# Rows of step 10 between step 11's scores, and expert 0's second half ahead of the fills of list and gates

## The chip, the cores and the metric

The kernel runs on one core of a Trainium2 chip. The metric is the device time of one execution in microseconds (us): the median of the runs of a kernel. Engines are named as in the profile: PE (TensorE, the matrix products), DVE (VectorE), ACT (ScalarE), POOL (GpSimd), SP (SyncE, which here only issues DMAs).

## What is computed

Three layers follow each other. A gated linear recurrence over 768 positions for 4 x 8 heads of 48 lanes; its rows, 3072 tokens of 384 values, go through a layer in which a score lets a token skip and an argmax sends every other token to one of eight experts; the result goes through a dense layer with SiLU.

```python
def _attn_ref(q, k, v, a_re, a_im):          # per batch and head, state S of 48 x 48
    ...
        S_re, S_im = (new_re + kv, new_im)   # decayed state plus outer product of k and v
        y[:, :, t] = np.einsum('bhd,bhde->bhe', q[:, :, t], S_re)

def _moe_ref(x, w_skip, w_gate, w1, w2):
    do_compute = x @ w_skip > 0
    xc = x[do_compute]
    logits = xc @ w_gate
    e_idx = np.argmax(logits, axis=1)
    ...                                      # gate_w: softmax of the chosen logit
    for e in range(E):
        mask = e_idx == e
        h = np.maximum(xc[mask] @ w1[e], 0.0)
        y[mask] = gate_w[mask, None] * (h @ w2[e])
    out[do_compute] = xc + y

def _moe2_ref(x, w_in, w_out):
    h = x @ w_in
    return ((h * (1.0 / (1.0 + np.exp(-h)))) @ w_out)
```

## The kernel before

The recurrence is worked in chunks of 128 positions. There are 12 steps: six chunks, each in two halves of two batches (b = 0 and 1). A step of attention ends with scores of keys and queries (`scores`, in four groups of four heads, `sc00`, `sc10` of batch 0, `sc01`, `sc11` of batch 1), a mask on DVE (`scores_out`), products with values and state (`value`), a copy `yT` on ACT (`value_out`), four transposes back to rows (`rows`, into the PSUM bank `px`), a copy `xr` (`rows_out`) and a DMA of these rows to the buffer xbuf in DRAM (`store`, on SP). After steps 1, 3, ... 11 the logits of the chunk are formed from `yT` (`logits`).

From the logits the router makes, on DVE and PE, a list: which token stands in which of 16 slots of 128 (two per expert). It does so in two parts, r0 for the first 16 groups of 128 tokens and r1 for the last 8. Per part: pick the expert (`e1`/`l1`), rank the token (a product), mark the slot, a one-hot matrix `hot` (`l4`), the fills of the list (`l6`, products slots<-r1bt,r1hot), the softmax weight (`y1` to `y6`) and the fills of the gates (`y7`, slots<-r1bg,r1hot). `slot_tokens` (`l7`) turns the list into `gidx`, by which POOL gathers the rows of each slot from xbuf.

Expert 0's first tile of 128 tokens comes from the list of r0 alone, and is worked inside the attention phase: `gather0`, `turn0`, up products of two halves in two pieces each (`up0`; `f4`, `p4` for the first half, `f5`, `p5` for the second), Relu on ACT (`relu0`; `f6`, `f8`), the low part on DVE (`relu0_lo`; `f7`, `f9`), products with the second weights (`down0`; `fa`, `pa`, each 12 products) and a copy `y0` (`fb`). The hidden values of the second half lie in the attention buffers cs and sn, those of the first in kn.

After it the expert phase begins (`dense`). Its first steps on PE: filler products on a matrix of ones (`idle`), the transposes of expert 0's second tile, again filler products, its up products (`up_one`) with the transposes of expert 1's two tiles between them, and its products `down_last`, which need Relu `hh` (ACT) and the low part `hl` (DVE). Weights of an expert come as four loads of 768 KB on SP (`load`), each cast on ACT (`whole`) and subtracted on DVE (`lower`). The two loads of expert 1's first weights go to a pool whose memory lies on the attention buffers; the second must wait until `down0` has read cs and sn.

What sets the order: within the attention phase each piece of work has a number in a table (PLACE, one for each of the 12 steps, and TAIL for the router and expert 0's first tile). All pieces are sorted by that number and written in that order, so every engine has its instructions in the order of the numbers. In the expert phase each piece has a due time worked out from a few constants, and the table SHIFT moves single ones. Each engine works strictly in its own order, and waits at an instruction until what it reads is there.

Of the kernel before, what the change touches and what calls it, by code (L numbers as in the profile page):

```python
# [105 lines left out]
    "flip": (0, 323, 0, 443, 0, 581, 0, 671, 0, 803, 0, 839),  # L106
    "lgb": (0, 344, 0, 462, 0, 632, 0, 677, 0, 805, 0, 841),
# [10 lines left out]
}  # L118
ENG = {
    "z": "VGVVVGGVGGVV", "qe": "VGGVGVVVGVVG", "ks": "GVVGVGGGVVVV", "kc": "GVVGGGVVVGVG", "qc":  # L120
# [18 lines left out]

SHIFT = {  # L140
# [4 lines left out]
}  # L145
# [1624 lines left out]
```

## Time and profile before

| | before |
|---|---|
| median of 3 runs | 775.18 us (774.18 to 775.31) |
| profiled execution | 778.0 us, span 776.2 us from first to last instruction |
| mean granted clock of PE | 0.988 of full |

The page gives for each engine its busy time. Below it the chain of work that ended last is followed back; most of it is PE. The rows shown further down are from views of the trace in order of time: start in us from the span's start, duration, engine, source line, operation, output and inputs with buffer numbers left out, count, and in brackets how long the engine sat idle before it and what ended that wait. A product of two float32 operands is recorded more than once, so counts of PE can be a multiple of those in the code.

### The profile page before, as it was taken

What the parts mean: (1) busy time and instruction counts of PE and PEld (TensorE: products, weight loads), DVE (VectorE), ACT (ScalarE), POOL (GpSimd) and SP (SyncE); (2) the same over time, 40 slices, a digit from 0 to 9 for tenths busy, and PEclk for the clock granted to TensorE, in tenths of its full rate; (3) what the DMA queues carried; (4) which work ended last, traced back from release to release, by engine and by line L of the source; (5) the groups of instructions that cost most, each with busy time, mean ns of one, the idle gap of its engine ahead of it and who ended that gap; (6) DMA issues with size and microseconds to landing.
All of it is one profiled execution on the core that took longest, in us unless ns stands there. A gap on an engine that the chain in (4) does not pass through costs nothing.

```text
span 776.2 us, 13953 instructions
## 1 busy us (share of the span) xinstructions
PE 741.5 (96%) x5499; PEld 683.1 (88%) x5499; DVE 536.1 (69%) x957; ACT 437.9 (56%) x718; POOL 211.0 (27%) x193
## 2 busy tenths in 40 slices
PE   3799999999999999999999999999999999999995
PEld 2699999998988999998999899988888888888885
DVE  7899889999754867579898243654565556556544
ACT  7899899955424654454676212344555455555443
POOL 4478567223523134224300037810000000000000
PEclk9799999999999999999999999999999999999998
DMA  8567787587837865657660011001000101101001
GB/s 345 166 199 234 243 267 235 158 230 224 277 108 274 293 238 211 225 202 229 213 215 34 1 41 41 1 31 44 9 30 12 42 1 41 41 1 42 1 1 45
DMA packets 31530, 101.87 MB, mean 131 GB/s; under 512 B 4960, under 2 KB 13536, under 8 KB 31456
## 3 DMA queue, kind: packets, MB, share of 16 engines
q1 hardware_dynamic: 26128, 88.05, 34.6%
q0 software_dynamic: 3072, 9.44, 3.3%
q10 hardware_dynamic: 2256, 3.41, 1.3%
q8 instruction: 45, 0.74, 0.4%
q14 instruction: 29, 0.24, 0.1%
HBM read 69.27 MB, written 12.58 MB: 105 GB/s over the span
## 4 chain that ended last, share of the span: by engine, by line
PE 78%; DMA 10%; DVE 3%; ACT 2%; issue 2%; SPq 2%; POOL 1%; DVEq 0%; POOLq 0%; ACTq 0%
PE ph L936 29%; PE py L936 25%; PE pd L936 6%; PE sc L483 4%; DMA xbuf<-xg,sidx 4%; DMA KQ<-o 3%; PE run L310 2%; PE pu L516 2%; PE py L501 2%; SPq L447 2%; PE py L505 2%; PE tp L473 1%; PE pt L1349 1%; PE px L533 1%; DMA raw<-in_w_dram 1%
## 5 line engine op out<-in xcount | busy, mean ns | idle before, releaser
L936 PE MATMUL ph<-cxh,wh 128*128 128x512 f32 x288 | 113.6, 395 | 0.0
L936 PE MATMUL ph<-cxl,wh 128*128 128x512 f32 x288 | 112.9, 392 | 0.0
L936 PE MATMUL ph<-cxh,wl 128*128 128x512 f32 x288 | 112.6, 391 | 0.0
L1214 DVE TENSOR_TENSOR gl<-g,gh 128x512 fp32r<-128x512 f32 x64 | 44.3, 692 | 89.1 <-ACT gh L1213 45.3
L1212 ACT ACTIVATE g<-ph 128x512 f32<-128x512 f32 x64 | 38.2, 597 | 49.4 <-PE ph L936 49.2
L936 PEld LDWEIGHTS ph<-cxl,wh 128*128 128x128 f32 x288 | 54.0, 188 | 11.6
L936 PEld LDWEIGHTS ph<-cxh,wl 128*128 128x128 f32 x288 | 54.1, 188 | 9.2
L936 PEld LDWEIGHTS ph<-cxh,wh 128*128 128x128 f32 x288 | 54.2, 188 | 9.0
L1234 ACT CAST tz<-twd 128x256 fp32r<-128x256 f32 x96 | 36.7, 407 | 42.2 <-DVE twd L1226 42.1
L1019 DVE TENSOR_TENSOR wl<-raw,wh 128x1536 fp32r<-128x1536 f32 x28 | 48.5, 1752 | 11.7 <-ACT wh L917 11.7
L483 PE MATMUL sc<-KQ 96*128 96x128 f32 x384 | 52.3, 285 | 0.0
L483 PEld LDWEIGHTS sc<-KQ 96*128 96x128 f32 x384 | 47.7, 198 | 1.6 <-issue 1.4
L917 ACT CAST wh<-raw 128x1536 fp32r<-128x1536 f32 x28 | 40.7, 1480 | 13.2 <-DMA raw<-in_w_dram 13.2
L936 PE MATMUL ph<-xh,wh 128*128 128x240 f32 x168 | 46.5, 277 | 0.0
L936 PE MATMUL ph<-xl,wh 128*128 128x240 f32 x168 | 46.1, 275 | 0.0
L936 PE MATMUL ph<-xh,wl 128*128 128x240 f32 x168 | 46.1, 275 | 0.0
L1051 POOL DMA_INDIRECT xbuf<-xg,sidx x16 | 21.7, 1356 | 84.5 <-DMA xbuf<-xg,sidx 41.4
L936 PE MATMUL py<-wh,gl 128*128 128x384 f32 x128 | 43.2, 338 | 0.0
L936 PE MATMUL py<-wh,gh 128*128 128x384 f32 x128 | 43.1, 337 | 0.0
L936 PE MATMUL py<-wl,gh 128*128 128x384 f32 x128 | 43.0, 336 | 0.0
L936 PE MATMUL py<-wh,hh 128*128 128x384 f32 (+1 forms) x120 | 41.7, 348 | 0.0
L936 PE MATMUL py<-wh,hl 128*128 128x384 f32 (+1 forms) x120 | 41.0, 342 | 0.4 <-DVE hl L1036 0.3
(374 smaller groups left out, 2117.4 us busy)
## 6 DMA issues: line engine op xcount, KB each, us to landing
raw<-in_w_dram SPq DMA_DIRECT2D x30, 768.0 KB, 5.9
KQ<-o SPq DMA_DIRECT2D x40, 290.2 KB, 3.8
kq<-in_kq_dram SPq DMA_DIRECT2D x12, 768.0 KB, 5.1
a<-in_a_dram SPq DMA_DIRECT2D x10, 768.0 KB, 6.5
raw<-in_w_in_dram SPq DMA_DIRECT2D x8, 768.0 KB, 4.9
raw<-in_w_out_dram SPq DMA_DIRECT2D x8, 768.0 KB, 4.3
v<-in_v_dram SPq DMA_DIRECT2D x12, 384.0 KB, 6.1
xbuf<-xr SPq DMA_DIRECT2D x24, 192.0 KB, 2.9
```

Source lines behind the costliest of these rows:

```text
L310: nc.tensor.matmul(p[:, i if bank is None else bank, g * CH:g * CH + CH], a[:, n * CH:n * CH + CH], tri, start=first and g == 0, stop=last ...
L447: nc.sync.dma_start(t.KQ[every(2 * d0 + half, n, 2), h0:h0 + ng, b], o[every(p0, n, step), g0:g0 + ng])
L483: nc.tensor.matmul(sc[:, j, :], key(4 * g + j), t.KQ[0:96, 4 * g + j, b, 1, 0:CH], start=True, stop=True)
L501: nc.tensor.matmul(py[64 * i:64 * i + 64, j, :], t.v[:, v0 + h * D:v0 + h * D + DP], u.P[:, h, :], start=True, stop=first)
L505: nc.tensor.matmul(py[64 * i:64 * i + 64, j, :], state[0:96, s0 + h * D:s0 + h * D + DP], t.KQ[0:96, h, b, 1, 0:CH], start=False, stop=True)
L917: nc.scalar.copy(hi, src)
L936: nc.tensor.matmul(out, a, x, start=first and n == 0, stop=last and n == len(pairs) - 1)
L1019: nc.vector.tensor_tensor(u.w[i][1], u.raw[i], u.w[i][0].bitcast(F32), ALU.subtract)
L1051: nc.gpsimd.indirect_dma_start(out=k.x, out_offset=bass.IndirectOffsetOnAxis(ap=k.sidx[:, c:c + 1], axis=0), in_=u.xg[i], in_offset=None)
L1212: nc.scalar.activation(a, u.ph[f], AF.Silu)
L1214: tt(u.gl[f], a, u.gh[f].bitcast(F32), ALU.subtract)
L1234: nc.scalar.copy(h, u.x[:, n])
```

## The change

Two groups of numbers are altered. Transposes, copy and store of step 10 (`row`, `xr`, `st`) get places among the scores of step 11, the deferred store of step 9 goes in front of them, and step 11's second rows and both its stores come a little earlier. In TAIL the second half of expert 0's first tile (`p5`, `f8`, `f9`, `pa`) gets places ahead of the fills of the list (`l6`, 868) and of the gates (`y7`, 878). In SHIFT the cast and the subtraction of expert 1's first load get 1.7 us more.

```diff
-    "row0": (211, 275, 327, 400, 502, 545, 610, 647, 721, 775, 862, 843),
-    "xr0": (233, 298, 329, 404, 520, 553, 616, 654, 727, 779, 864, 845),
-    "st0": (316, 469, 446, 432, 543, 668, 624, 748, 787, 865, 876, 863),
+    "row0": (211, 275, 327, 400, 502, 545, 610, 647, 721, 775, 817.5, 843),
+    "xr0": (233, 298, 329, 404, 520, 553, 616, 654, 727, 779, 817.7, 845),
+    "st0": (316, 469, 446, 432, 543, 668, 624, 748, 787, 830.1, 830.2, 852),
...
-    "row1": (204, 258, 373, 408, 522, 560, 704, 684, 742, 784, 846, 857),
-    "xr1": (210, 267, 390, 421, 539, 562, 709, 703, 753, 789, 851, 861),
-    "st1": (378, 407, 482, 505, 667, 577, 729, 736, 764, 802, 855, 881),
+    "row1": (204, 258, 373, 408, 522, 560, 704, 684, 742, 784, 822.5, 846),
+    "xr1": (210, 267, 390, 421, 539, 562, 709, 703, 753, 789, 822.7, 851),
+    "st1": (378, 407, 482, 505, 667, 577, 729, 736, 764, 802, 830.4, 855),
...
-    867, "l6": 868, "p5": 869, "f7": 870, "f8": 871, "l7": 872, "y6": 873, "yb": 874, "fa": 875, "f9": 877,
-    "y7": 878, "y8": 879, "pa": 880, "fb": 882,
+    867, "l6": 868, "p5": 862.5, "f7": 870, "f8": 863.5, "l7": 872, "y6": 873, "yb": 874, "fa": 875, "f9": 872.5,
+    "y7": 878, "y8": 879, "pa": 876.5, "fb": 882,
...
-    "E1 lower 3": 2, "E1 relu_lo 0": 1, "E1 whole 1": 0.2, "E2 lower 1": 4.65, "E2 turn 0": -0.4,
+    "E1 lower 0": 1.7, "E1 lower 3": 2, "E1 relu_lo 0": 1, "E1 whole 0": 1.7, "E1 whole 1": 0.2, "E2 lower 1": 4.65, "E2 turn 0": -0.4,
```

On PE, at the scores sc of step 11 (KQ_144 are its keys and queries, px the transposes to rows):

```order
 L505 MATMUL py<-KQ_143,state 64x128 x2
-L483 MATMUL sc<-KQ_144 128x128 x16
+L483 MATMUL sc<-KQ_144 128x128 x4
+L533 MATMUL px<-ident,yT 128x128 x4
+L483 MATMUL sc<-KQ_144 128x128 x8
+L533 MATMUL px<-ident,yT 128x128 x4
+L483 MATMUL sc<-KQ_144 128x128 x4
 L501 MATMUL py<-P_2581,v_139 64x128 x2
```

The two groups of transposes of step 10 now stand behind the first and the third group of scores.

On PE, where the list is filled (slots<-r1bt,r1hot; ph_2747 and ph_2760 are the second half up of expert 0's first tile, py its products, of which the first rows are shown):

```order
-L533 MATMUL px<-ident,yT 128x128 x4
-L926 MATMUL ph_2747<-KQ_143,raw 128x128 x6
-L533 MATMUL px<-ident,yT 128x128 x4
+L926 MATMUL ph_2760<-KQ_143,raw 128x128 x12
 L836 LDWEIGHTS r1hot
 L836 MATMUL slots<-r1bt,r1hot 128x32
...
-L926 MATMUL ph_2747<-KQ_143,raw 128x128 x6
-L936 MATMUL py_2802<-wh,kn_2745 128x384
...
+L936 MATMUL py_2806<-wh,kn_2758 128x384
```

Both pieces of the second half up stand in front of the fills of the list, and no transposes are left there. The 24 products py now follow the list's fills in one piece, and the fills of the gates, which stood between the first and the second 12, come behind them.

On ACT, from the last copies of rows to the Relu hh of expert 0's second tile (y is the copy of the first tile's result, xh the second tile's rows, wh the casts of expert 1's first two loads):

```order
-L248 COPY xr_2755<-px 128x384
-L248 COPY xr_2763<-px 128x384
-L658 ACTIVATE cs<-ph_2747 128x512
-L705 COPY y_68<-py_2802 128x384
-L917 CAST wh<-raw 128x1536
+L658 ACTIVATE cs<-ph_2760 128x512
+L705 COPY y_68<-py_2806 128x384
 L1061 COPY xh<-pt 128x3x128
-L917 CAST wh<-raw 128x1536
+L917 CAST wh<-raw 128x1536 x2
 L1071 ACTIVATE hh<-ph 128x512
```

The copy xh now stands ahead of both casts, and hh behind both, as before.

On DVE the low part sn of the second half moves from behind the chain of the gates to a place right behind gidx. On SP the five stores of rows keep their place between the loads of expert 0's and expert 1's weights; their order among themselves changes from step 10, 11, 9, 10, 11 to 9, 10, 10, 11, 11. POOL's order stays.

## Rows read from the trace of the kernel before

**Rows 1.** The page, part 1: busy time, share of the span, instructions

```profile
PE 741.5 (96%) x5499; PEld 683.1 (88%) x5499; DVE 536.1 (69%) x957; ACT 437.9 (56%) x718; POOL 211.0 (27%) x193
```

**Rows 2.** PE in order of time, 214 to 233 us: start, duration, work

```profile
214.25 0.55 PE L649 MATMUL tp<-ident,xg 128*128 128x128 f32 x3
...
223.60 0.66 PE L533 MATMUL px<-ident,yT 128*128 128x128 f32 x4 [0.41 <-ACT xr L248]
224.09 1.50 PE L926 MATMUL ph<-KQ,raw 128*128 128x128 f32 x12
225.43 0.60 PE L533 MATMUL px<-ident,yT 128*128 128x128 f32 x4
225.87 0.59 PE L836 MATMUL slots<-r1bt,r1hot 128*128 128x32 bf16 x8
...
227.64 0.42 PE L936 MATMUL py<-wh,kn 128*128 128x384 f32 x1
...
229.82 0.37 PE L836 MATMUL slots<-r1bg,r1hot 128*128 128x48 bf16 x8
230.03 0.42 PE L936 MATMUL py<-wh,cs 128*128 128x384 f32 x1
...
232.24 0.95 PE L983 MATMUL pt<-ones 128*128 128x128 bf16 x14
```

**Rows 3.** DVE in order of time, 224 to 230 us

```profile
224.85 1.29 DVE L827 TENSOR_TENSOR r1hot<-i,r1rest 128x512 bf16<-128x512 f32 x2
...
226.84 0.17 DVE L867 TENSOR_TENSOR gidx<-base,slots 128x16 uint32<-128x16 f32 x1
...
228.92 0.56 DVE L791 TENSOR_TENSOR r1bg<-r1oc,r1g 128x384 bf16<-128x384 f32 x1
```

**Rows 4.** SP's queue in order of time, 232 to 234 us

```profile
232.43 0.34 SPq L1013 DMA_DIRECT2D raw<-in_w_dram  x1
```

**Rows 5.** POOL in order of time, 207 to 233 us: gathers

```profile
207.31 1.18 POOL L642 DMA_INDIRECT xg<-xbuf,gidx  x1 [0.52 <-DVE gidx L861]
...
229.80 0.97 POOL L990 DMA_INDIRECT xg<-xbuf,gidx  x1 [14.43 <-DVE r1bg L791]
...
232.32 0.94 POOL L990 DMA_INDIRECT xg<-xbuf,gidx  x1 [0.30 <-issue]
```

**Rows 6.** DMA issues at 207.3, 227.4, 232.43, 232.3 us: size, us to landing

```profile
xg<-xbuf,gidx POOLq DMA_INDIRECT x1, 5.9
...
raw<-in_w_dram SPq DMA_DIRECT2D x1, 768.0 KB, 4.2
...
raw<-in_w_dram SPq DMA_DIRECT2D x1, 768.0 KB, 6.3
xg<-xbuf,gidx POOLq DMA_INDIRECT x1, 6.6
```

**Rows 7.** ACT and DVE in order of time, 238 to 243 us

```profile
238.78 1.47 ACT L917 CAST wh<-raw 128x1536 fp32r<-128x1536 f32 x1 [4.12 <-DMA raw<-in_w_dram]
...
242.02 0.68 DVE L931 SCALAR_TENSOR_TENSOR hl<-ph,hh 128x512 fp32r<-128x512 f32 x1
```

**Rows 8.** PE in order of time, 234 to 243 us: expert 0's second tile

```profile
234.72 2.94 PE L926 MATMUL ph<-xh,raw 128*128 128x128 f32 x24 [0.30 <-ACT xh L1061]
...
239.07 0.52 PE L1002 MATMUL pt<-ident,xg 128*128 128x128 f32 x3 [1.08 <-DMA xg<-xbuf,gidx]
...
242.03 0.42 PE L936 MATMUL py<-wh,hh 128*128 128x384 f32 x1
...
242.76 0.44 PE L936 MATMUL py<-wh,hl 128*128 128x384 f32 x1
```

**Rows 9.** PE in order of time, 360 to 361 us: group 0's transposes

```profile
360.70 1.39 PE L1349 MATMUL pt<-ident,xr 128*128 128x128 f32 x6 [1.41 <-DMA xr<-xbuf,order]
```

**Rows 10.** Two stretches: length, busy by engine, granted clock, DMA share, GB/s

```profile
236.00:244.00 8.00, 6.77 (x54) 6.25 (x54) 3.78 (x6) 3.32 (x5) 2.84 (x3) 1.00 0.76 244
360.00:366.00 6.00, 5.21 (x22) 5.02 (x23) 4.79 (x8) 3.06 (x5) 1.72 (x2) 0.72 0.42 165
```

## The prediction

> **What bounds the kernel now.** The page comes first: TensorE (PE) is busy for 741.5 us [rows 1] of a span of 776.2, so only work taken off PE, or a wait of PE, can move the end; DVE, ACT and POOL matter through the waits that they cause. The change takes no product away, so the question is which waits of PE it ends. Second view, PE in order of time in the stretch that the change edits, from the last scores of attention to expert 0's second tile. Three places are to be seen there. PE waits 0.41 us in front of the transposes at 223.60, for ACT to empty the bank px. The products py of expert 0's first tile begin at 227.64, are cut by the fills of the gates (229.82 to 230.03), and the next work begins at 232.24 [rows 2]. Behind that PE waits 0.30 us for ACT's xh, 1.08 us for a gather, and at the second tile's products it starts the first at 242.03 but the third only at 242.76 [rows 8].
>
> Third, what stands behind that last wait. SP issues the second load of expert 1's weights at 232.43 [rows 4], the moment at which the products py of the first tile end: the load's buffer lies on cs and sn, which these products read. It lands 6.3 us later [rows 6], ACT casts it at 238.78 with all later work of ACT behind it, and DVE's hl, which the third product needs, begins at 242.02 [rows 7]. So the chain is: end of py, load 6.3, then 238.75 to 242.76, 4.0 us of cast, subtraction and hl. PE has work in parallel, but less of it than this chain is long. The end of py decides.
>
> **The change, part by part.** The time that I work against is the profiled execution's, 776.2 us of span and 778.0 in all; the runs shown have a median of 775.18. The saving in us is put on that median.
>
> *Rows of step 10 between the scores.* Two groups of four transposes px move from behind (225.43 to 225.87 is 0.44 each [rows 2]) to between the four groups of scores. PE has no wait there, so everything behind them, up to the transposes of step 11, is 0.88 later. The logits are among it, and so the whole list chain on DVE: its last step, r1hot, ended at 224.85 + 1.29 = 226.14 [rows 3] and will end at 227.02.
>
> What it gives: the transposes of step 11 no longer share the bank px with step 10's in that stretch, so the wait of 0.41 goes. PE starts expert 0's second half up at 224.09 + 0.88 - 0.44 - 0.41 = 224.12, as before (224.09 is where the transposes of 223.60 ended). Now both pieces run in one, 2 x 1.34 (224.09 to 225.43 [rows 2]), to 226.80. The first four list fills take 0.2, and PE comes to the second four at 227.0, when r1hot is just there. The cover is used up exactly: any later r1hot is a wait of PE. The fills end at 227.3, products py start at 227.35 instead of 227.64: 0.29 earlier.
>
> *Relu and subtraction of the second half earlier, products in one piece.* Relu on ACT follows the up products at 226.8, sn on DVE follows gidx and ends near 228.5; PE needs it 2.2 us after 227.35, at 229.5. No wait. The chain of the gates on DVE is pushed back by the 0.88 and by sn (0.6 in line): r1bg ended at 229.48 [rows 3] and ends near 231.0. PE comes to these fills at 227.35 + 2 x 2.2 = 231.75, so again nothing, with 0.7 us to spare. As these fills (0.21, 229.82 to 230.03 [rows 2]) now stand behind the products and not in them, the products end 0.29 + 0.21 = 0.50 earlier: the second load leaves at 231.93 instead of 232.43.
>
> *Stores earlier.* SP's queue was held by the first of five stores until step 11's rows were copied; now three of them leave during step 11's scores, beside the gather of the first tile. That gather left at 207.31 [rows 5] and took 5.9 [rows 6], so it was there at 213.2, and PE wanted it at 214.25, now at 215.1 [rows 2]. Below: no loss. Above: the slowest gather among my rows took 6.6 [rows 6], which gives 213.9. No cost. The other gathers waited for the last of these stores to land. It now leaves near 224.4 (step 11's transposes end at 223.75, the copy takes 0.5) and has 3.5 us until the list is there, so they wait for the list alone: gidx ends at 227.01 + 0.88 = 227.9, the first gather leaves at 228.2 instead of 229.80, the third (expert 1's second tile) 2.5 later, 230.7 instead of 232.32 [rows 3, 5]. Even with its 6.6 us it is there at 237.3; PE would want it at 239.07 - 1.08 - 0.30 - 0.29 = 237.4. The wait of 1.08 ends.
>
> *Cast of expert 1's first half behind xh on ACT.* ACT took the cast (1.47 [rows 7]) first and xh behind it; with the order turned, xh is ready while PE still runs its filler products, and the 0.30 goes. The cast itself has no reader before the subtraction on DVE, 2 us before the next one needs DVE.
>
> *What is late next.* PE's own work from 232.24 to 242.03 is 9.79 less the waits 0.30 and 1.08, 8.41. From 231.95 it is at the second tile's products at 240.36, and without a wait the third would be at 240.8. But hl comes by the chain: 231.93 + 6.3 + 4.0 = 242.26. Of the 1.38 us saved on the way nothing reaches the end; PE waits them again, as one wait of some 1.5 us, and the third product is 0.50 earlier than before.
>
> The one price that the rows of before don't fix is the second load's landing. It took 6.3 with gathers leaving 0.1 before it and every 1.25 us behind it; the first load of the pair took 4.2 [rows 6]. After the change the gathers are 1.6 earlier and the load 0.5, so again one leaves at almost the same moment (231.95) and others follow at the same pace. The nearest row is thus the load itself, and I take 6.3; bounds are 4.2 and 7 (a little over the 6.6 of the gather beside it).
>
> The Trainium skill (DMA: Bandwidth & Descriptors, section on the anatomy of one DMA) gives a fixed 2.0 us plus bytes over 436 GB/s, by which I estimate 3.8 us for these 768 KB. The first load's 4.2 nearly agrees, the second's 6.3 does not, and by the page's figure alone hl would not be what PE waits for, as in the second case below.
>
> Sum: 0.50 us earlier at the third product. Behind it I see no wait of PE that is worth a term until the 1.41 at 360.70 [rows 9], and loads, casts and scatters there are started by work that moves along. 775.18 - 0.50 = 774.7; the profiled execution by the same sum has a span of 775.7.
>
> **The rivals.**
>
> *The load lands sooner.* If it is back in 4.2 us, it lands at 236.1 and hl is ready at 240.1, before PE comes. Then PE alone decides, and the third product is at 240.8, 1.96 earlier: 773.2. For it: fewer gathers are left to follow the load, since they began 1.6 earlier, and expert 2's load is held longer by the later subtraction. Against it: at 231.95 the fourth gather leaves just as the third did at 232.32.
>
> *The gain is taken back later.* At 360.70 PE has waited 1.41 us for the last gather of group 0's rows [rows 9], which ends POOL's long chain of scatters and gathers, each waiting for a landing. If that chain keeps its time while PE comes 0.5 earlier, PE waits 0.5 longer there, and the time is 775.2. The same comes out if r1hot or the load is half a us late. Against it: expert 1's scatters start that chain, and they follow PE.
>
> *A clock that falls.* Behind that wait of 1.41 the granted clock fell from 2.4 to 1.2 GHz for a while: the mean over 360 to 366 is 0.72, so 6 x 0.28 = 1.7 us of full clock were lost. From 236 to 244 it stayed at 1.00 [rows 10], with the 1.08 of rows 8 as the longest wait. The change joins the waits into one of 1.5, longer than the one that was followed by the fall. If the clock falls there too, the time is 774.7 + 1.7 = 776.4, slower than before; with a load of 7 us the wait grows to 2.2 and the time to 777.1. [...] Against it: around that one PE had another wait and only a few transposes, here products stand on both sides.
>
> That the change doesn't do what it says I give no weight of its own: if r1hot is so late that the products don't begin earlier, it is the second rival.
>
> **How the numbers follow.** Forecast 0.50, at 774.7 (774.2 to 775.2 for a landing of 5.8 to 6.8); sooner landing 0.23, at 773.2; taken back 0.14, at 775.2; clock 0.13, at 776.4. 0.2% is 1.55 us, about what a measurement of this kernel can tell from no change: faster means below 773.6, slower above 776.7. The sooner landing gives nearly all of faster, 0.22; of the clock's case about half, with a late load, goes over the upper bound, and some part of what I have not seen: 0.09; the rest, 0.69, is within. The range is 773.0 to 776.5: it takes in the full gain below and a fall of the clock above.
>
> **What would show it.** Right: the transposes of step 10 stand between scores; no wait for xr behind the rank; products py in one piece from about 227.3; the second load issued near 231.9; no wait for the gather; one wait of about 1.5 us inside the second tile's products, ended by hl; the third product near 242.3. Wrong: a landing of that load under 5.5 or over 7 us; a wait of more than 0.3 us for r1hot or r1bg; a granted clock below 1 between 236 and 250; a wait at group 0's transposes that differs by more than 0.5 us from before.

## The result and the profile after

| | before | after |
|---|---|---|
| median, 13 runs each | 775.18 us (773.73 to 777.03) | 780.14 us (775.74 to 783.39) |
| ratio, 95% interval | | 1.0058 (1.0043 to 1.0073) |
| profiled execution: span | 776.2 us | 777.9 us |

By the medians the change makes the kernel 5 us slower, where 0.5 us faster was forecast (774.7, range 773.0 to 776.5). In this set its runs also spread more than twice as far; in a later set the kernel before spread as far, from 771.7 to 780.7. A ratio is the measurement's own, over the runs that were not disturbed, and can differ a little from the quotient of two medians.

The page of after, part 1, answers [rows 1]: PE has the same work.

```profile
PE 742.3 (95%) x5499; PEld 684.3 (88%) x5499; DVE 538.1 (69%) x957; ACT 437.9 (56%) x718; POOL 208.8 (27%) x193
```

PE of after in order of time, from the scores of step 11 to the third product of expert 0's second tile; it answers [rows 2, 8].

```profile
209.79 0.60 PE L533 MATMUL px<-ident,yT 128*128 128x128 f32 x4
...
212.01 0.60 PE L533 MATMUL px<-ident,yT 128*128 128x128 f32 x4
...
223.52 0.60 PE L533 MATMUL px<-ident,yT 128*128 128x128 f32 x4
...
224.12 2.92 PE L926 MATMUL ph<-KQ,raw 128*128 128x128 f32 x24
226.88 0.67 PE L836 MATMUL slots<-r1bt,r1hot 128*128 128x32 bf16 x8
...
227.40 0.42 PE L936 MATMUL py<-wh,kn 128*128 128x384 f32 x1
...
231.81 0.37 PE L836 MATMUL slots<-r1bg,r1hot 128*128 128x48 bf16 x8
232.03 0.94 PE L983 MATMUL pt<-ones 128*128 128x128 bf16 x14
232.80 0.50 PE L1002 MATMUL pt<-ident,xg 128*128 128x128 f32 x3
233.14 0.94 PE L983 MATMUL ph<-ones 128*128 128x128 bf16 x14
239.64 5.22 PE L926 MATMUL ph<-xh,raw 128*128 128x128 f32 x24 [5.56 <-ACT xh L1061]
...
247.95 0.42 PE L936 MATMUL py<-wh,hh 128*128 128x384 f32 x1
...
248.38 0.35 PE L936 MATMUL py<-wh,hl 128*128 128x384 f32 x1
```

Down to 233.14 it goes as forecast. Then PE sits for 5.56 us in front of the second tile's up products, waiting for ACT's copy xh, where it waited 0.30 before. The products themselves take 5.22 us instead of 2.94. The third product comes at 248.38, 5.62 later than in before.

Who held xh up: ACT, DVE, SP and POOL of after in order of time.

```profile
232.01 0.48 ACT L705 COPY y<-py 128x384 f32<-128x384 f32 x1 [4.26 <-issue]
239.11 0.48 ACT L1061 COPY xh<-pt 128x384 f32<-128x384 f32 x1 [6.62 <-remote]
...
233.28 0.21 DVE L875 TENSOR_REDUCE gate<-slots 128x16 f32<-128x48 f32 x1 [1.91 <-PE slots L836]
...
232.00 0.34 SPq L1013 DMA_DIRECT2D raw<-in_w_dram  x1
...
228.99 0.97 POOL L990 DMA_INDIRECT xg<-xbuf,gidx  x1 [13.78 <-DVE r1ex L724]
...
236.53 0.95 POOL L990 DMA_INDIRECT xg<-xbuf,gidx  x1 [0.30 <-issue]
```

ACT was free at 232.49 and the transposes that xh reads had their recorded end at 233.30, yet ACT started at 239.11, "remote". DVE shows the same on a smaller scale: the fills of the gates ended at 232.18 and their reader started at 233.28. The chain of waits of after (the view goes from 224 to 262 us) has no better name for it:

```profile
232.01 0.48 ACT y L705
232.49 6.56 another core or an unknown queue
239.04 0.03 ACTq L1061
...
239.11 0.49 ACT xh L1061
```

The trace also lists when PE's signal (the semaphore that ACT, DVE and SP wait for) counted up: at 233.25 and at 239.04, in place of 232.18 and 233.30. So the work was done and its signal came late, by 1.07 and 5.74 us. In before these two were 0.02 late. PE, ACT and DVE of before show their readers: gate follows the fills of [rows 2], which end at 230.19, at once, and xh follows the cast ahead of it, half a us behind the transposes.

```profile
233.09 0.55 PE L1002 MATMUL pt<-ident,xg 128*128 128x128 f32 x3
...
232.81 1.48 ACT L917 CAST wh<-raw 128x1536 fp32r<-128x1536 f32 x1
234.18 0.48 ACT L1061 COPY xh<-pt 128x384 f32<-128x384 f32 x1
...
230.23 0.21 DVE L875 TENSOR_REDUCE gate<-slots 128x16 f32<-128x48 f32 x1
```

The Trainium skill (Perfetto Trace Analysis, section Tensor Engine Instruction) says that PE's reported end is an estimate, and that the signal is pushed after PSUM's acknowledgement and then has to spread, outside the profiled part. The trace agrees on where the time is hidden, between that end and the signal.

Two stretches of after (length, busy by engine, granted clock, DMA share, GB/s) answer [rows 10]:

```profile
236.00:244.00 8.00, 4.36 (x20) 4.36 (x21) 2.60 (x2) 3.22 (x3) 1.18 (x2) 0.60 0.33 115
...
360.00:366.00 6.00, 6.00 (x52) 5.79 (x52) 5.93 (x9) 4.28 (x7) 0.55 (x1) 1.00 0.89 316
```

The clock fell to 1.2 GHz while PE sat idle, and stayed there for most of the up products (from 237.6 to 244.4 us by the trace's list of clock changes): their 5.22 against 2.94 are another 2.3 us. At 360 us, on the other hand, there is neither the wait of [rows 9] nor its fall of the clock: 3.8 us came back there in this execution. That is why the two profiled executions differ by 1.7 us only. The medians differ by 5, because the profiled execution of before (778.0) lies 2.8 us above the median of its kernel, while that of after (779.58) lies 0.6 below. All 13 executions of before in the table were shorter than the one whose rows are shown, and no trace shows where: that of e13, the same kernel, is of 779.12.

### The profile page after: what moved, and what is told of

Read it like the earlier page. It is cut to its first block, busy times and chain, and to the rows that moved or that the text cites. A ratio compares the mean times of both kernels' runs of the same rounds, so it can differ in the third digit from the quotient of the medians.

```text
span 777.9 us, 13956 instructions
## 1 busy us (share of the span) xinstructions
PE 742.3 (95%) x5499; PEld 684.3 (88%) x5499; DVE 538.1 (69%) x957; ACT 437.9 (56%) x718; POOL 208.8 (27%) x193
## 4 chain that ended last, share of the span: by engine, by line
PE 83%; DVE 6%; ACT 3%; DMA 3%; issue 2%; SPq 1%; another core or an unknown queue 1%; POOL 0%; DVEq 0%; ACTq 0%; POOLq 0%
PE ph L936 32%; PE py L936 27%; PE pd L936 6%; PE sc L483 4%; PE pu L516 2%; PE run L310 2%; PE py L501 2%; DMA KQ<-o 2%; PE py L505 2%; PE ph L926 1%; PE tp L473 1%; PE px L533 1%; PE pt L1349 1%; DMA a<-in_a_dram 1%
## 5 line engine op out<-in xcount | busy, mean ns | idle before, releaser
L1051 POOL DMA_INDIRECT xbuf<-xg,sidx x16 | 23.7, 1479 | 94.0 <-DVE xg L1047 29.2
L1213 ACT CAST gh<-g 128x512 fp32r<-128x512 f32 x64 | 39.8, 621 | 2.0
```

Source lines behind the costliest of these rows:

```text
L1051: nc.gpsimd.indirect_dma_start(out=k.x, out_offset=bass.IndirectOffsetOnAxis(ap=k.sidx[:, c:c + 1], axis=0), in_=u.xg[i], in_offset=None)
L1213: nc.scalar.copy(u.gh[f], a)
```

## The experiments

In the comparisons "the stretch" is the time from the scores of step 11 (203 us) to expert 1's up products (251 to 255 us) against the trace of before: the median difference in start of the same instructions at its two ends. In after it is +6.07. It leaves out the start-up and what happens at 360, which differ from run to run. It is one execution's, and a median of some ten need not follow it. Of changed lines of SHIFT the edits show the entries that differ, and the definitions of the buffers `hold` and `ones4`, with the uses of `idle` that pass whole tiles, are left out.

**e1, the change again.** No edit.

> The changed kernel once more, for a second trace of the place where PE sat idle for 5.56 us (ahead of the up products of expert 0's second tile, for the copy xh on ACT) while the transposes that xh reads stood in the trace 5.7 us earlier, and after which the granted clock fell to half. If the idle time belongs to this order of work, it comes again at the same place with 4 us or more, with the half clock behind it, and the time is 778 to 782. If it was one accident of that one execution, xh follows the transposes within 0.3 us, PE is at the third product of that tile near 242.3, and the time is 774 to 776.

Measured: 780.18 (778.14 to 783.69), before 775.58; ratio 1.0056 (1.0031 to 1.0081). The same wait, 5.6 us; the signals 1.07 and 5.78 late; stretch +4.48. It came in both traces of this order of work.

**e2, casts first.**

```diff
-    "E1 lower 0": 1.7,
-    "E1 whole 0": 1.7,
```

> The change without its two entries in SHIFT: expert 1's first cast stands ahead of xh on ACT again. Theory 1 (the order on ACT makes xh late): the idle time shrinks to the 0.30 us of before, the time is 774.5 to 775.5. Theory 2 (PE reports its transposes late because the fills of the gates, the fillers and the transposes now follow each other directly): the idle time stays at 4 us or more, but the cast runs in it, so the time is 777 to 781. Theory 3 (loads and gathers crowd, because the gathers leave 1.6 us earlier): the idle time stays as well.

Measured: 776.08, ratio 1.0003 (0.9976 to 1.0030). PE's wait is still 4.2 us, the signals 1.05 and 4.34 late, stretch +4.47. The order on ACT is not the cause: theory 1 falls by the trace, while the median lies between the two expectations. This execution got 4.0 us back at 360. Of the ten runs five lie at 772.9 to 774.9 and five, the profiled one among them, at 777.2 to 780.3; whether the first five had the late signal isn't known.

**e3, rows only.** The kernel before with the new numbers of row, xr and st alone.

> The kernel before with the places of the rows and stores of steps 9 to 11 changed, and nothing else. Theory 1: no idle time over 1.5 us, 775 to 776. Theory 2: none either, since the products py still stand between the fills of the gates and the fillers; 775 to 776 (0.88 us paid for the two groups of transposes, the wait of 0.41 gone, the gathers earlier). Theory 3: the gathers leave earlier here too, so the idle time of 4 us or more is here, and the time is 777 to 781.

Measured: 778.84, ratio 1.0033 (1.0000 to 1.0065); stretch +5.96. Here the fills stand between the products, as in before, and their signal is in time; the one behind the products is 1.27 late, that of the transposes 4.52. Theory 2, which needs fills, fillers and transposes in a row, falls.

**e4, first tile only.** The kernel before with the new p5, f8, f9, pa alone.

> The kernel before with the four changed places of expert 0's first tile alone (second half up, its Relu, its low part and its products ahead of the fills), rows and stores as before. Theory 1: no idle time over 1.5 us, 774.5 to 775.5. Theory 2: the idle time of 4 us or more is here, 777 to 781. Theory 3: the gathers leave when they left before, so no idle time, 774.5 to 775.5.

Measured: 778.18, ratio 1.0038 (1.0011 to 1.0066); stretch +4.99. PE's signals are in time (0.01). But on ACT the last copy of step 10's rows (`xr0`, 864) now stands behind the Relu of the second half (`f8`, 863.5), which waits for all up products: it starts at 229.21, in before at 226.07. So the last stores leave 3 us later, the first gather leaves at 232.92, and PE waits 4.2 us for it. No theory had foreseen this; it is a wait of its own, not the late signal.

**e5, no fillers.**

```diff
-        for _ in range(14):
+        for _ in range(0):
```

> The changed kernel without its 28 filler products ahead of expert 0's second tile. In the traces of the change, PE's signals behind these rows of small products reach ACT and DVE late (fills of the gates 1.07 us, transposes 5.7 us after their recorded end), and many semaphore events of that stretch are missing. Theory N (rows of small products one behind the other hold PE's signals up): without them the transposes end near 232.6, xh follows within 0.1 us, no wait over 1.6 us, up products of the second tile start near 233.2, time 773.5 to 776. Theory G (seven gathers and a load, that now leave earlier, stall what stands behind them): the late signal stays at 4 us or more, time 778 to 782.

Measured: 775.00, ratio 0.9981 (0.9950 to 1.0013); stretch -1.35, of which 0.8 is lost again by 257 us. PE and ACT of e5:

```profile
231.72 0.55 PE L1002 MATMUL pt<-ident,xg 128*128 128x128 f32 x3 [0.15 <-issue]
234.73 2.94 PE L926 MATMUL ph<-xh,raw 128*128 128x128 f32 x24 [2.46 <-ACT xh L1061]
237.51 0.82 PE L1002 MATMUL pt<-ident,xg 128*128 128x128 f32 x6
238.17 2.84 PE L926 MATMUL ph<-xh,raw 128*128 128x128 f32 x24
...
234.20 0.48 ACT L1061 COPY xh<-pt 128x384 f32<-128x384 f32 x1 [2.33 <-remote]
...
238.63 0.60 ACT L1071 ACTIVATE hh<-ph 128x512 fp32r<-128x512 f32 x1
```

The late signal shrinks (1.86) but doesn't go, between the two theories. What is new stands at 237.5: the up products and the two groups of transposes end at 237.68, 238.00 and 238.33, and their three signals come at 238.60, 238.66 and 238.71. Work that ends 0.32 and 0.33 us apart can't be signalled 0.06 and 0.05 apart unless the signals had queued: it is they that are held, not PE.

**e6, large fillers.**

```diff
-        for _ in range(14):
-            nc.tensor.matmul(x, k.ones, k.ones, start=True, stop=True)
+        for _ in range(14 // x.shape[1]):
+            nc.tensor.matmul(x, k.ones, k.ones4[:, 0:x.shape[1]], start=True, stop=True)
```

> The changed kernel with 4 filler products of 384 columns and 3 of 512 in place of 14 and 14 of 128: nearly the same busy time of PE in a quarter of the instructions. Theory N: no late signal or one under 1 us, since the number of instructions is what counts; 774 to 776. Theory G: the late signal stays at 4 us or more, 778 to 782.

Measured: 776.57, ratio 1.0007 (0.9982 to 1.0033); stretch +2.13; signals 1.06 and 2.97 late. A quarter of the instructions halves the delay; theory N alone doesn't explain it.

**e7, gathers late.**

```diff
+    "E2 gather 0": 25, "E2 gather 1": 24.1, "E3 gather 0": 23.2, "E3 gather 1": 22.3,
```

> The changed kernel with the four gathers of experts 2 and 3 moved behind the first scatter, at about 250 us, so that only three gathers and the load are under way from 229 to 239 us. Theory N: the late signal stays at 4 us or more, 778 to 782. Theory G: it goes, or shrinks by half at least, and the time is 774 to 777.

Measured: 787.15, ratio 1.0136 (1.0091 to 1.0182). The late signal is nearly gone: 0.11 us, with all 28 fillers. The time is lost further on, where PE waits 11.3 us for the gathers that I put behind a scatter. Theory G holds for the signal; my price for the move did not.

**e8, before without fillers.** The edit of e5 on the kernel before.

> The kernel before without the 28 filler products. Theory N: nothing much to win, since its signals came in time; PE would wait for the gather instead of running fillers; 774.5 to 776.5. Theory G: the same, 774.5 to 776.5. It shows what the fillers are worth in the order of before.

Measured: 776.13, ratio 1.0004 (0.9976 to 1.0033); stretch +0.13. As expected: worth nothing either way there. But in its trace PE waited 0.77 us for the gather and 1.00 for xh with the transposes between, the clock was at 1.2 GHz from 235.7 to 239.1, and the second tile's up products took 4.57 us.

**e9, four gathers held.** A copy of one column of hh on POOL, ahead of the four gathers of experts 2 and 3.

```diff
-            at(6.5, down_last)
+            at(6.5, down_last); at(3.0, lambda: nc.gpsimd.tensor_copy(k.hold, u.hh[0][:, 0, 0:1].bitcast(F32)))
...
+    "E2 gather 0": 19.2, "E2 gather 1": 18.3, "E3 gather 0": 17.4, "E3 gather 1": 16.5,
```

> The changed kernel, with the four gathers of experts 2 and 3 held on POOL until the first Relu hh of expert 0's second tile (a copy of one column of hh on POOL stands ahead of them). Theory G (PE's signals come late while a row of seven gathers is under way): xh follows the transposes within 0.2 us, no wait over 1.6 us, third product of the second tile about 1 us earlier than before, relative to the scores of step 11; time 773.5 to 775.5. Theory N (the row of 28 small filler products does it): the late signal of 4 us or more stays, 778 to 782.

Measured: 775.03, ratio 1.0001 (0.9976 to 1.0025). Signals 0.34 and 0.09 late, xh behind the transposes at once. The stretch, +0.32, holds a wait of 1.55 for the first tile's gather.

**e10, held longer.** The same with `u.hh[1]` at 5.8, and the gathers 2.8 us later still in the table.

> The same with the four gathers held until the second Relu hh, some 3 us later. Theory G: as the one before up to the third product; the gathers of expert 2 then leave near 242 and land by 250, ahead of their transposes at 256, so again 773.5 to 775.5; if they come late PE waits for them near 256. Theory N: 778 to 782.

Measured: 776.28, ratio 1.0014 (0.9987 to 1.0041); the profiled execution has a span of 770.9. Signals 0.34 and 0.08 late. PE, ACT and SP of e10:

```profile
232.21 0.50 PE L1002 MATMUL pt<-ident,xg 128*128 128x128 f32 x3
...
233.39 2.94 PE L926 MATMUL ph<-xh,raw 128*128 128x128 f32 x24
...
241.04 0.44 PE L936 MATMUL py<-wh,hl 128*128 128x384 f32 x1 [0.98 <-DVE hl L931]
...
232.86 0.48 ACT L1061 COPY xh<-pt 128x384 f32<-128x384 f32 x1 [0.97 <-PE pt L1002]
...
237.07 1.47 ACT L917 CAST wh<-raw 128x1536 fp32r<-128x1536 f32 x1 [2.36 <-DMA raw<-in_w_dram]
...
231.41 0.34 SPq L1013 DMA_DIRECT2D raw<-in_w_dram  x1
```

This is the profile that the prediction had described: xh in time, the up products without a wait, one wait for hl. At 203 us this execution was 0.78 ahead of before, so its third product, 241.04, is 0.94 earlier than 242.76 beyond that. Of this 0.65 is the second load, which landed in 5.63 us instead of 6.28 [rows 6] with four gathers fewer about it. Behind it PE waits 0.6 for expert 2's held gather, and the stretch ends at -0.12.

**e11, two gathers held.** Expert 3's alone.

> The changed kernel with only the two gathers of expert 3 held until the first Relu hh; five leave in one row. If the delay of the signals grows with the number of gathers in the row, it lies between 0.1 us (three) and 4.4 to 5.8 us (seven): 1 to 3 us, time 775 to 778. If it needs all seven it is gone, 773.5 to 775.5; if more than three are enough for all of it, 778 to 782.

Measured: 780.88 in 4 runs, ratio 1.0084 (1.0056 to 1.0111); stretch +2.28. PE and ACT of e11:

```profile
231.84 0.50 PE L1002 MATMUL pt<-ident,xg 128*128 128x128 f32 x3
...
235.88 4.46 PE L926 MATMUL ph<-xh,raw 128*128 128x128 f32 x24 [2.76 <-ACT xh L1061]
...
235.35 0.48 ACT L1061 COPY xh<-pt 128x384 f32<-128x384 f32 x1 [3.83 <-remote]
```

With five gathers in the row the transposes' signal is 2.94 late: between three (0.1) and seven (5.7), the top of the expected 1 to 3. The time is not the expected 775 to 778: the profiled run, 775.16, is the fastest of the four, the others lie at 780.1 to 784.5, and what they lost isn't known.

**e12, before with four held.** The edit of e9 on the kernel before.

> The kernel before with the four gathers held in the same way. If the hold helps by itself, by sooner landings of the third gather and the second load, PE's wait of 1.08 us for that gather goes and the time is 773.5 to 775. If it only takes away what the change brought, 774.5 to 776, as the kernel before.

Measured: 774.04, ratio 0.9984 (0.9969 to 0.9998). But the trace speaks against the reason given: the third gather landed later, not sooner, and PE waited 2.3 us for it (stretch +2.94), and the transposes' signal was 0.51 late, hidden by the cast that stands ahead of xh.

**e13, before again.** No edit.

> The kernel before once more, for a second trace. If the time of PE's signals belongs to the order of work, the signals of its seven gathers' stretch (fills of the gates, products, transposes) are again within 0.1 us of their recorded ends, and the wait for xh is again near 0.3 us. If it is chance, a late signal of over 1 us is found here too. Apart from that: whether the waits of 0.28 and 1.41 us at group 0's transposes, and the half clock behind them, are there in each execution.

Measured: 779.12 in one run; signals 0.02 late, xh's wait 0.3, as in before; stretch -0.13. PE's waits of e13 (us in total, times, longest) show the place at 360 again:

```profile
PE pt L1349 <- DMA xr<-xbuf,order: 2.3, 2, 1.4
...
PE ph L926 <- ACT xh L1061: 0.3, 1, 0.3
```

**e14, all seven later.** The copy on POOL reads the softmax weights and stands ahead of all seven gathers.

```diff
+ at(end, "yb", lambda: nc.gpsimd.tensor_copy(k.hold, late.gate[:, 0:1]), shift=-1e-4)
```

> The changed kernel with all seven gathers held together until the softmax weights of the second list are done (a copy of one of its columns on POOL), some 1.8 us later, at about 230.8 instead of 229.0. If it matters how far the row of seven has come when PE signals the fills of the gates and the transposes, the transposes' signal is under 1 us late; PE waits up to 1.5 us for the first gather instead, and the time is 774.5 to 776.5. If seven gathers in a row are enough wherever they start, the signal comes 3 us late or more, and the time is 778 to 782.

Measured: 777.79, ratio 1.0048 (1.0025 to 1.0071); stretch +2.83. PE and ACT of e14:

```profile
237.12 0.55 PE L1002 MATMUL pt<-ident,xg 128*128 128x128 f32 x3 [3.92 <-DMA xg<-xbuf,gidx]
...
237.75 0.48 ACT L1061 COPY xh<-pt 128x384 f32<-128x384 f32 x1 [5.04 <-PE pt L1002]
```

Both signals are in time (0.02), as the first expectation had it, but the time lies 0.2 short of the second's: the first gather, issued at 231.60, took 5.5 us to land, and PE waited 3.92 for it. The first gathers of before took 3.2. In this trace it is a landing that is late, not a signal. That the later row put the signals in time isn't shown: this trace is one of the five with nearly all their records, which have no late signal at all (see the table below).

**e15, held and no fillers.** The edits of e10 and e5 on the change.

> The changed kernel with the four gathers of experts 2 and 3 held until the second Relu hh, and without the 28 fillers. By theory G the signals are in time, PE is at the second tile's products 1.7 us sooner than with the fillers, but waits there for hl, whose chain starts at the second load; the third product comes where it came with the fillers, 1.2 to 1.4 us earlier than before. Time 773.5 to 775.5. If the idle time in one piece (2.5 to 3 us) lets the clock fall, 1 to 2 us more.

Measured: 773.04, ratio 0.9977 (0.9946 to 1.0009); signals 0.01 late, waits of 0.6 for xh, 1.3 for hl and twice 0.4 for the held gathers, the clock at full, stretch +0.03. Against the scores at 203 us the third product (242.19) is 0.52 earlier than in before, not the expected 1.2 to 1.4.

**e16, before held again.** e12 once more.

> The kernel before with the four gathers held until the first Relu hh, timed again in more rounds: 774.04 against 775.44 the first time. If that was real, 773.5 to 774.5 against 775.2 to 775.8 for the kernel before; if it was chance, within 0.5 us of it.

Measured: 773.31 against 774.72, ratio 0.9996 (0.9973 to 1.0019), stretch -1.24. Two medians of 1.4 less, one interval below 1 and one around it: a gain of over 0.2% isn't shown.

**e17, e15 again.**

> The changed kernel with four gathers held and without fillers, timed again: 773.04 against 774.72 the first time, with an interval of 0.9946 to 1.0009. If the change is worth what its trace shows once the late signals are gone, about 1.2 us at the third product, the time is again 1 to 2 us under the kernel before.

Measured: 776.70, ratio 0.9992 (0.9964 to 1.0021): the lead of e15 was not repeated. Stretch +1.69; with three gathers alone the signals were 1.04 and 0.43 late again. PE, SP and POOL of e17:

```profile
216.87 0.55 PE L649 MATMUL tp<-ident,xg 128*128 128x128 f32 x3 [2.71 <-DMA xg<-xbuf,gidx]
...
359.47 0.49 PE L1349 MATMUL pt<-ident,xr 128*128 128x128 f32 x2
361.52 0.33 PE L1349 MATMUL pt<-ident,xr 128*128 128x128 f32 x1 [1.56 <-DMA xr<-xbuf,order]
362.48 1.33 PE L1349 MATMUL pt<-ident,xr 128*128 128x128 f32 x5 [0.63 <-DMA xr<-xbuf,order]
...
207.77 4.45 SPq L542 DMA_DIRECT2D xbuf<-xr  x3
...
206.76 1.18 POOL L642 DMA_INDIRECT xg<-xbuf,gidx  x1 [0.49 <-DMA KQ<-o]
```

and the same place of e15, PE in order of time:

```profile
358.42 1.04 PE L1349 MATMUL pt<-ident,xr 128*128 128x128 f32 x8
```

Two traces of one kernel, 5.4 us apart in span: 4.3 of them arise at 360, where e17 waits twice and loses its clock, and e15 does neither. In e17 the first tile's gather was 2.71 us late as well, with the stores of the change leaving SP right behind it.

**e18, before held, no fillers.** The edits of e9 and e5 on the kernel before.

> The kernel before with four gathers held and without fillers: the same two edits on the old places. If the rows between the scores and the products in one piece are worth 0.5 us or more by themselves, this one is slower than e17 by 0.5 to 1.5 us; if all the gain lies in the hold, the two agree within 0.5 us.

Measured: 775.52, ratio 0.9992 (0.9961 to 1.0023), stretch -1.13. That is 1.2 under e17, where 0.5 to 1.5 more or the same within 0.5 was expected. With the crowd gone the old order is no worse than the new one; no version beats the kernel before by more than the measurement can tell.

The signals in one table (us between PE's recorded end and its signal, from the trace's list of signals; a star: that signal isn't in the list, and the start of its reader stands in its place, in e8 and e18 behind a cast and so as an upper bound). The last column is how many landings of DMAs the trace has recorded:

| kernel | gathers in the row | fillers | fills of the gates | transposes | landings recorded |
|---|---|---|---|---|---|
| before, e13 | 7 | 28 | 0.02 | 0.02 | 4959, 4960 |
| e8 (before) | 7 | none | 0.01 | 0.47* | 4821 |
| e12, e16 (before) | 3 | 28 | 0.01, 0.02 | 0.51, 0.01 | 4827, 4960 |
| e18 (before) | 3 | none | 0.01 | 0.32* | 4841 |
| e4, first tile only | 7 | 28 | 0.01 | 0.01 | 4842 |
| e3, rows only | 7 | 28 | 0.02 | 4.52 | 4807 |
| after, e1 | 7 | 28 | 1.07, 1.07 | 5.74, 5.78 | 4812, 4807 |
| e2 | 7 | 28 | 1.05 | 4.34 | 4806 |
| e6 | 7 | 7 large | 1.06 | 2.97 | 4786 |
| e5 | 7 | none | 0.40* | 1.86 | 4783 |
| e11 | 5 | 28 | 1.09 | 2.94 | 4832 |
| e7, e9, e10 | 3 | 28 | 0.04*, 0.34, 0.34 | 0.11, 0.09, 0.08 | 4835, 4822, 4849 |
| e15, e17 | 3 | none | 0.01, 1.04 | 0.01, 0.43 | 4955, 4823 |
| e14 | 7, the first 2.4 us later against the fills | 28 | 0.01 | 0.02 | 4959 |

## Why the prediction was wrong

*Rows between the scores, first tile in one piece: right.* Second half up at 224.12 (forecast 224.12), fills 226.88 (227.0), products 227.40 (227.35), second load 232.00 (231.93). That the clock times agree so closely is luck: at the scores (203 us) this execution was 0.56 ahead of before, and at 209.46 it waited 0.65 for keys (KQ), a wait that the trace of before lacks and that of e13 has too (0.5). Without both the second load comes at 231.91, so the sum holds. The waits of 0.41 [rows 2] and 1.08 [rows 8] are gone. The first gather left at 228.99, not 228.2: 0.88 us behind gidx, where 0.3 had been taken.

*"xh is ready while PE still runs its filler products": this step failed.* It took for granted that a signal arrives when its work ends, as the rows of before show it. When PE ended its transposes (233.30), the fourth of the seven gathers had just left (232.78) and the other three followed 1.25 us apart; the signal of the transposes was 5.74 us late, and PE's wait for xh went from 0.30 to 5.56. e2 clears the order on ACT, e3 shows that the new places of rows and stores bring it, e7, e9 and e10 that it goes when four of the seven gathers stay away (the same fills' and transposes' signals were still 1.04 and 0.43 late in e17), and e9, e10, e15 and e17 that the 5 us of the medians go with it (ratios 0.9977 to 1.0014). Not every median follows the trace, though: e2 and e6 had late signals in theirs and are no slower (1.0003, 1.0007), so how many executions of a kernel have the late signal isn't known. That five gathers lie between (e11) and that the fillers add to it (e5, e6) rests on one trace each. I had counted the earlier gathers as pure gain, and asked of the crowd only how long the load would take to land.

*The clock.* It fell, as in the third rival, but behind a wait that no case had. The wait of 1.3 us for hl that I feared (e7 1.29, e15 1.3) left it at full. The length of one wait doesn't settle it in these traces: behind 0.77 and 1.00 us with the transposes between (e8) it fell for 3.4 us, behind 2.46 (e5) and 2.71 (e17, at 216.87) it stayed at full.

*The chain behind the second load: right in kind.* In e10 load to cast took 5.66 (I took 6.3), cast to third product 3.97 (4.0), and the wait for hl is there, 0.98. The 3.8 us estimated for that load from the Trainium skill (DMA: Bandwidth & Descriptors, section on the anatomy of one DMA) are too little there too; the section fits its figures to DMAs that GpSimd issues, and this load is issued by SP. The third product was 0.94 earlier in e10 and 0.52 in e15, where 0.50 was forecast; in e10 the load left only 0.24 earlier than in before, and the rest is its sooner landing. So the sum was about right for a kernel whose signals come in time and four of whose gathers stay away; the change itself is not such a kernel.

*Stores earlier, "no cost": wrong at times.* In e6, e9 and e17 PE waited 0.55, 1.55 and 2.71 us for the first tile's gather. I had bounded the landing by 6.6; in e17 it took 10 (206.76 to 216.87). In the seven traces with the old places of the stores it took 4.7 to 7.0, and one of them (e4) has a wait of 0.4 too; in the thirteen with the new places 4.5 to 10.1.

*Group 0.* The second rival looked at the right place with the wrong picture: against the trace of before, the way from 347 to 372 us is -0.01 to +0.61 in five of the other traces, -3.6 to -4.1 in thirteen and -1.1 in one (e5). Whether PE waits there, and then runs at half clock, differs between executions of one kernel (after and e1, e15 and e17), and it is a good part of the spread of the times. The three traces of the old order with its seven gathers (before, e8, e13) all have it and the three with four held (e12, e16, e18) don't, so an edit may shift the odds; that isn't settled, since those three executions (778.0, 779.23, 779.12) are among the longest of their kernels.

*The range* had no case for a late signal, so it ended at 776.5.

What stays open: which path holds the signals, whether POOL's issuing or the transfers themselves load it, and what else it needs. The number of gathers under way isn't all of it: at the recorded end of the transposes before and after had both issued four of the seven, the first of them 3.83 and 4.31 us earlier, and before's signal was in time. Executions differ too. The five traces with nearly all records of landings (before, e13, e14, e15, e16) have no signal over 0.02 late. The fifteen others lack a hundred or more each, and all eleven of them with the new places of rows and stores have a signal that is 0.1 to 5.8 late. e15 and e17 are one kernel, e12 and e16 another, and in each pair only the trace with missing records has late signals.

So whatever loses the records goes along with the late signals. It may be the recording itself, which then would be part of the delay: every timed run lists a span and a granted clock, so none is known to have gone without it. Or it may be the chip: e13 to e16 ran on one chip, and no trace of the change itself from that chip is on record. Neither was tested. The comparisons that carry the account stay among traces with missing records: seven gathers against three in the new order (after and e1 against e7, e9 and e10), and the new order against the old without fillers, in one set (e5 1.86, e8 at most 0.47).

## What to carry to other kernels

When a change makes a row of transfers leave earlier, price what else happens while they are all under way: signals between engines, not only landings. A start "remote" or an "unknown queue" in the chain, with the work it waits for long ended, is the sign; compare the start of the reader with the recorded end of the work. Look at a second trace of the same kernel before a stretch is credited to an edit: here one place was worth 4 us in one execution and nothing in the next.

## What was not expected of the hardware

PE's signals followed its recorded ends by 0.02 us in the traces of before; in the changed order, with seven gathers of 192 KB and a load of 768 KB under way, they came up to 5.78 late, and in e5 three of them 0.06 and 0.05 apart. One load of 768 KB took 4.2 us when it left 2.4 us ahead of the gathers [rows 5, 6], and 5.66 to its cast beside three gathers (e10). An idle PE of 5.56 us brought 6.8 us at 1.2 GHz, one of 2.32 us (e12) 3.4 us, one of 2.46 us (e5) none.
